# Expert weight sums formed once, ahead of time, and kept in DRAM, with deeper buffers for the expert weights

## The chip, the cores and the metric

The kernel runs on one core of a Trainium2 chip. The engines of the core are named as the profile names them: PE (TensorE; PEld is its weight load), DVE (VectorE), ACT (ScalarE), POOL (GpSimd) and SP (SyncE, which here only issues DMA transfers). The metric is the device time of one execution in microseconds (us), and less is better.

## The reference, cut to what matters

```python
attn = attention(q, k, v, mask from the nearest of 16 centroids)   # 2 x 8 heads, 768 tokens, head size 64
x = attn.transpose(0, 2, 1, 3).reshape(1536, 512)
x = softplus(x @ w_in) @ w_out                                     # w_in 512 x 2048
P = 8 rounds of Sinkhorn scaling of exp(x @ w_gate - max)          # 1536 x 8
for e in range(8):                                                 # the expert stage
    h = maximum(x @ w1[e], 0)                                      # w1[e] 512 x 1024
    out += P[:, e:e+1] * (h @ w2[e])                               # w2[e] 1024 x 512
```

## The kernel before

The program has three stages, one after the other. Attention comes first. It works through 8 pairs of heads in a list of events with hand-set step numbers (24 steps to a pair), and each pair is prepared ahead of its use: split into parts, compared with the centroids, and the cluster masks formed. The first feed-forward stage follows, in 16 units of 128 columns (`m1`, line 53). Then comes the expert stage, with 16 rounds k: 8 experts for each half of the tokens.

In the expert stage the tokens' matrix and each expert's weights are cut in 2 x 2 blocks and multiplied by the seven products of Strassen's method in Winograd's form. `PROD` (line 106) lists them: the token side is a block (A11...) or a sum of blocks (S1 to S4), the weight side a block (B11, B21, B22) or a sum (T1 to T4). Every operand is split into a high part that TensorE's fast 32-bit format holds exactly (`h`, a cast on ACT) and the rest (`l`, a subtraction), and each product takes three matmuls in place of one.

- First matrix (`x @ w1`): a round has four units u, each with 128 of the 512 half columns. `w1_load` (line 751) brings the four blocks of a unit to `wf`, one buffer of seven slots; `w1_sum` (761 to 763) forms T1 to T4 in it on POOL; `w1_split` (765) casts on ACT (`whA`, `whB`, `whC`, line 770) and subtracts on DVE (`wlA`, `wlB`, `wlC`, line 771), in three pieces: A holds B11 and B21, B holds T1 and T2, C holds the rest. `l1_group` (827) does the matmuls of one product (line 843, tiles `l0m`, `l1m`, `l3m`), copies partial sums out of PSUM on ACT (`c00m`, `c22m`, `c03m`, line 852) and adds on DVE (`XA`, line 862).
- Second matrix (`h @ w2`): `w2_load`, `w2_sum` (POOL, line 795), `w2_split` (ACT line 800, POOL line 801, tiles `vh` and `vl`), `g_split` for the token side (`gh`, `gl`, lines 821 and 822), and `l2_piece` for the matmuls (line 878, tiles `Y`).

The order is set by a list of events: `do(t, fn)` gives each step a time in units of one product of the first matrix (28 to a round), and the steps are written out sorted by it. The recording layer then moves instructions on each engine, by priorities and its own estimate of what is ready. At run time each engine works through its own row strictly in order, SP with its DMA issues too; a semaphore holds an instruction until its operands are there and its target is free. The loads of a unit stand 7.5 and 6.4 units ahead of its first product.

In attention `pair_argmax` (line 365) forms the cluster masks of a pair: DVE, then POOL (`A`, line 379), DVE, POOL (`OH`, line 387), and `pair_ohT` (390) transposes them on PE (`po`, line 394).

## Time and profile before

| | |
|---|---|
| median of 3 runs | 1773.78 us (1773.32 to 1778.39) |
| the profiled execution's own time | 1769.33 us |
| its span, first to last instruction | 1767.5 us |
| busy share of PE, DVE, ACT, POOL | 89%, 74%, 56%, 55% |
| mean granted TensorE clock | 0.958 of full speed |
| read from and written to HBM | 93.44 MB and 3.15 MB |

Time outside the span is 1.8 us. The busy shares are means over three stages with different limits, so the rows further down are taken by stage.

### The profile page before, as it was taken

How to read it: one execution, taken by the hardware profiler on the slowest of the kernel's cores; microseconds unless marked ns; L12 is line 12 of the kernel's file. 1: busy time of each engine (PE TensorE's matmuls, PEld its weight loads, DVE VectorE, ACT ScalarE, POOL GpSimd, SP SyncE). 2: the span in 40 equal slices, each digit the busy share in tenths (PEclk: the TensorE clock that was granted, in tenths of full speed). 3: DMA queues.
4: the chain of work that ended last, by engine and by line, in shares of the span. 5: the costliest groups of instructions: out<-in, count | busy, mean ns of one | idle time of the engine just before them, and what ended most of it. 6: DMA issues, size and time to landing. Idle time of an engine off the chain costs nothing.

```text
span 1767.5 us, 26385 instructions
## 1 busy us (share of the span) xinstructions
PE 1565.5 (89%) x9873; PEld 1488.7 (84%) x9873; DVE 1305.2 (74%) x1899; ACT 997.4 (56%) x1822; POOL 976.3 (55%) x760
## 2 busy tenths in 40 slices
PE   5899998999999988888988889878888988888798
PEld 4788887999997788888988888777888988888798
DVE  5899988876636788776766767877676777667678
ACT  4788887665654545455544545544555454554454
POOL 3323243211223357767667766775767677677676
PEclk8999999999999999999998999899999999999999
DMA  7564410311200111212111111112211112111110
GB/s 203 156 163 136 96 27 25 119 56 65 72 19 13 47 55 54 66 55 60 55 54 60 58 62 55 42 60 84 66 54 60 54 54 66 54 60 54 55 54 37
DMA packets 127985, 118.74 MB, mean 67 GB/s; under 512 B 6896, under 2 KB 115568, under 8 KB 127856
## 3 DMA queue, kind: packets, MB, share of 16 engines
q1 hardware_dynamic: 127712, 116.99, 22.3%
q8 instruction: 77, 1.26, 0.3%
q14 instruction: 52, 0.43, 0.1%
q10 hardware_dynamic: 144, 0.07, 0.0%
HBM read 93.44 MB, written 3.15 MB: 55 GB/s over the span
## 4 chain that ended last, share of the span: by engine, by line
PE 37%; POOL 23%; DVE 14%; DMA 10%; issue 9%; ACT 7%; SPq 0%; DVEq 0%; POOLq 0%; ACTq 0%
POOL wf L763 11%; DMA wf<-in_moe_w_dram 9%; PE y L639 7%; PE p L605 7%; POOL vl L801 5%; POOL w2t L795 4%; PE l0m L843 4%; PE av L507 3%; PE s L452 2%; PE t L492 2%; POOL w2r L795 2%; PE l3m L843 2%; PE Yb0m L878 2%; DVE gl L822 2%; PE Ya0m L878 2%
## 5 line engine op out<-in xcount | busy, mean ns | idle before, releaser
L763 POOL TENSOR_TENSOR wf<-wf 128x256 f32<-128x256 f32 x256 | 255.0, 1016 | 102.3 <-DMA wf<-in_moe_w_dram 50.4
L801 POOL TENSOR_TENSOR vl<-w2r,vh 128x512 fp32r<-128x512 f32 x128 | 205.5, 1607 | 171.4 <-ACT vh L800 171.4
L822 DVE TENSOR_TENSOR gl<-XA,gh 128x768 fp32r<-128x768 f32 x160 | 200.9, 1257 | 71.8 <-ACT gh L821 71.5
L801 POOL TENSOR_TENSOR vl<-w2t,vh 128x512 fp32r<-128x512 f32 x96 | 154.7, 1612 | 128.5 <-ACT vh L800 128.2
L770 ACT CAST whAm<-wf 128x512 fp32r<-128x512 f32 x64 | 39.6, 619 | 260.5 <-DMA wf<-in_moe_w_dram 258.1
L821 ACT CAST gh<-XA 128x768 fp32r<-128x768 f32 x160 | 133.6, 835 | 76.0 <-PE Yb1m L878 38.9
L771 DVE TENSOR_TENSOR wlAm<-wf,whAm 128x512 fp32r<-128x512 f32 x64 | 46.8, 732 | 152.4 <-ACT whAm L770 152.3
L878 PE MATMUL Ya0m<-vh,gl 128*128 128x256 f32 x512 | 146.1, 285 | 1.4 <-DVE gl L822 1.4
L878 PE MATMUL Ya0m<-vl,gh 128*128 128x256 f32 x512 | 145.7, 285 | 0.0
L878 PE MATMUL Ya0m<-vh,gh 128*128 128x256 f32 x512 | 145.6, 284 | 0.0
L843 PE MATMUL l3m<-chS,whCm 128*128 128x384 f32 x128 | 52.1, 407 | 83.1 <-ACT c03m L852 83.1
L864 ACT ACTIVATE XA<-XA 128x768 f32<-128x768 f32 x96 | 81.0, 845 | 63.8 <-DVE XA L862 63.8
L878 PE MATMUL Yb0m<-vh,gh 128*128 128x256 f32 x384 | 110.0, 287 | 2.3 <-DVE x L896 2.3
L878 PE MATMUL Yb0m<-vh,gl 128*128 128x256 f32 x384 | 110.2, 287 | 0.7 <-DVE gl L822 0.7
L878 PE MATMUL Yb0m<-vl,gh 128*128 128x256 f32 x384 | 110.1, 287 | 0.0
L499 DVE TENSOR_TENSOR el<-t,eh 128x384 fp32r<-128x384 f32 x192 | 102.4, 549 | 9.9 <-ACT eh L495 8.7
L771 DVE TENSOR_TENSOR wlCm<-wf,whCm 128x768 fp32r<-128x768 f32 x64 | 78.9, 1233 | 40.5 <-ACT whCm L770 40.2
L460 DVE TENSOR_REDUCE sc<-s 128x1 f32<-128x768 f32 x96 | 91.1, 950 | 20.0 <-PE s L452 19.8
L495 ACT CAST eh<-t 128x384 fp32r<-128x384 f32 x192 | 91.2, 480 | 20.8 <-PE t L492 11.8
L843 PEld LDWEIGHTS l3m<-chS,whCm 128*128 128x128 f32 x128 | 27.4, 214 | 88.7 <-ACT c03m L852 88.5
L795 POOL TENSOR_TENSOR w2t<-w2r,w2t 128x512 f32<-128x512 f32 x64 | 99.1, 1549 | 5.4 <-DMA w2r<-in_moe_w_dram 1.7
L492 PE MATMUL t<-idf,E 128*128 128x128 f32 x576 | 97.6, 276 | 4.7 <-ACT OHT L400 2.8
(242 smaller groups left out, 5790.2 us busy)
## 6 DMA issues: line engine op xcount, KB each, us to landing
w2r<-in_moe_w_dram SPq DMA_DIRECT2D x64, 512.0 KB, 3.6
wf<-in_moe_w_dram SPq DMA_DIRECT2D x128, 256.0 KB, 2.7
AT<-HL SPq DMA_DIRECT2D x64, 192.0 KB, 3.9
r<-in_moe_w_in_dram SPq DMA_DIRECT2D x16, 512.0 KB, 4.4
r<-in_moe_w_out_dram SPq DMA_DIRECT2D x16, 512.0 KB, 4.3
Bt<-HL SPq DMA_DIRECT2D x32, 192.0 KB, 3.8
rT<-in_qt_dram SPq DMA_DIRECT2D x8, 384.0 KB, 3.2
rT<-in_kt_dram SPq DMA_DIRECT2D x8, 384.0 KB, 3.7
```

Source lines behind the costliest of these rows:

```text
L492: nc.tensor.transpose(pt[:, t * P : (t + 1) * P], Et[i, t][:, s * P : (s + 1) * P], idf)
L499: nc.vector.tensor_tensor(el, TT.pop((i, s)), EHL[i, s].bitcast(F32), ALU.subtract)
L605: nc.tensor.matmul(ps, wt[:, s_, ks], xx[:, k_, :], start=n == 0, stop=n == 6 * nk - 1)
L639: nc.tensor.matmul(o_, wt[:, q, ms], gt[:, cols], start=first and i == 0 and st, stop=last and i == 2, skip_group_check=True,)
L763: nc.gpsimd.tensor_tensor(wf[:, SLOT[name], :], wf[:, SLOT[a], :], wf[:, SLOT[b], :], ALU.subtract)
L771: nc.vector.tensor_tensor(l, src, h.bitcast(F32), ALU.subtract)
L795: nc.gpsimd.tensor_tensor(W2R[name][p], W2R[a][p], W2R[b][p], ALU.subtract)
L801: nc.gpsimd.tensor_tensor(l, src, h.bitcast(F32), ALU.subtract)
L821: nc.scalar.copy(h, src)
L822: nc.vector.tensor_tensor(l, src, h.bitcast(F32), ALU.subtract)
L843: nc.tensor.matmul(ps, wt[:, s_, ks], xx[:, k_, :], start=i in (0, 1, 3) and n == 0, stop=n == 3 * nk - 1, skip_group_check=True,)
L878: nc.tensor.matmul(ps, g[:, v, ts], w[:, v, :], start=i in (0, 1, 3) and p == 0 and v == 0 and n == 0 and t != 1, stop=p == 1 and v == 1 a ...
```

## The change

The sums T1 to T4 depend on the weights alone, and the kernel before forms them in every round. The new version forms them once. `t_load` brings the four blocks of one expert and unit to a tile `ts`, `t_sums` makes T1 to T4 in place with four subtractions on POOL, and `t_store` writes them to a DRAM tile (`TD[0]` for w1, `TD[1]` for w2). There are 32 such groups for w2, in attention (one every 4.9 steps from step 24 on), and 32 for w1, in the first feed-forward stage (one every 3.2 products).

In the expert stage `w1_load` and `w2_load` then read blocks from the inputs and sums from the DRAM tiles. The raw weights of the first matrix have two buffers (`WR[0]` in `wf`, `WR[1]` in new tiles `w1r`), loaded 12, 11 and 10 units ahead; those of the second have four half buffers in turn. The subtraction of piece C (`wlC`) goes from DVE to POOL. Nothing else in the expert stage's arithmetic changes.

```diff
@@ new, ahead of the first feed-forward stage's helpers
+    def t_load(pool, m, e, u):
+        t = TS[m, e, u] = slot_pool[pool].tile([P, 4, KC // 2 * P], F32, tag="ts", name=f"ts{m}_{e}_{u}", bufs=TSB[pool])
+        for fh in range(2):
+            o = fh * (FE // 2) + u * P
+            if m:
+                nc.sync.dma_start(t[:, 2 * fh : 2 * fh + 2, :].rearrange("p s d -> p (s d)"), w2[e, o : o + P, :])
+            else:
...
+    def t_sums(m, e, u):
+        t = TS[m, e, u]
+        b11, b12, b22, b21 = (t[:, n, :] for n in ((0, 1, 3, 2) if m else (0, 1, 2, 3)))
+        for o_, u_, v_ in ((b11, b12, b11), (b12, b22, b12), (b22, b22, b11), (b21, b21, b22)):
+            nc.gpsimd.tensor_tensor(o_, u_, v_, ALU.subtract)
+
+    def t_store(m, e, u):
+        nc.sync.dma_start(TD[m][e][u], TS.pop((m, e, u)))
+
+    TSB = {"ap": 3, "fp": 2}
@@ in attention's events
+    for n in range(E * NF2):
+        e, u = divmod(n, NF2)
+        t = 24 + 4.9 * n
+        at(t, lambda e=e, u=u: t_load("ap", 1, e, u), ("tl", 0))
+        at(t + 6, lambda e=e, u=u: t_sums(1, e, u), ("tq", 0))
+        at(t + 12, lambda e=e, u=u: t_store(1, e, u), ("tw", 0))
@@ the expert stage
-    def w1_sum(name):
-        a, b = BSUMS[name]
-        nc.gpsimd.tensor_tensor(wf[:, SLOT[name], :], wf[:, SLOT[a], :], wf[:, SLOT[b], :], ALU.subtract)
+        if ch == "A":
+            nc.sync.dma_start(
...
+        elif ch == "B":
+            nc.sync.dma_start(dst[0], TD[0][e][u][:, 0:4:2, :])
+        else:
...
+            nc.sync.dma_start(dst[0][:, 1:3, :] if len(dst) == 1 else dst[1], TD[0][e][u][:, 1:4:2, :])
...
-        nc.scalar.copy(h, src)
-        nc.vector.tensor_tensor(l, src, h.bitcast(F32), ALU.subtract)
+        n = 0
+        for src in WR[u % 2, ch]:
+            m = src.shape[1]
+            hs = h[:, n : n + m, :]
+            nc.scalar.copy(hs, src)
+            (nc.gpsimd if ch == "C" else nc.vector).tensor_tensor(l[:, n : n + m, :], src, hs.bitcast(F32), ALU.subtract)
+            n += m
...
-    def w2_sum(k, name, p):
-        a, b = BSUMS[name]
-        nc.gpsimd.tensor_tensor(W2R[name][p], W2R[a][p], W2R[b][p], ALU.subtract)
+        else:
+            n = TORD[1].index(name)
+            for u in range(NF2):
+                nc.sync.dma_start(dst[:, u, :], TD[1][e][u][:, n, :])
...
-                do(t0 - 7.5, w1_load, k, u, 0)
-                do(t0 - 6.4, w1_load, k, u, 1)
-                for n, name in enumerate(("T1", "T2", "T3", "T4")):
-                    do(t0 - 4.5 + 0.3 * n, w1_sum, name)
+                for ch, d in (("A", -12), ("B", -11), ("C", -10)):
+                    do(t0 + d, w1_load, k, u, ch)
...
+        for i in range(7):
+            b, i_ = divmod(7 * k + i - 4, 7)
+            do(split_at[b][2 * i_ + 1] + 0.15 if b >= 0 else -1, w2_load, k, i)
@@ in the first feed-forward stage
+    for m in range(E * NF2):
+        e, u = divmod(m, NF2)
+        for o, fn in ((0, lambda e=e, u=u: t_load("fp", 0, e, u)), (3, lambda e=e, u=u: t_sums(0, e, u)),
+                      (5, lambda e=e, u=u: t_store(0, e, u))):
+            tsum_at.setdefault(divmod(int(3.2 * m) + o, 7), []).append(fn)
```

Line numbers grow with the new functions: 770 becomes 814, 771 becomes 815, 852 becomes 896, 379 becomes 405, 387 becomes 413.

ACT's row in the expert stage before, from the first to the fourth product of a unit (`whAm_0` is piece A of the next round's unit 0, `whBm_3` piece B of unit 3, `c03m_2` the copy in unit 2):

```order
L852 COPY c00m_2_11013<-l0m_2_11006 128x384
L821 CAST gh_51_11079<-XA_1_10436 128x768
L800 CAST vh_51_11075<-w2r_6563 128x512
L852 COPY c22m_2_11064<-l0m_2_11006 128x384
L770 CAST whAm_0_11265<-wf 128x512
L770 CAST whBm_3_11139<-wf 128x512
L852 COPY c03m_2_11104<-l3m_2_11097 128x384
```

The same place in ACT's row of the new version:

```order
L896 COPY c00m_2_11671<-l0m_2_11664 128x384
L814 CAST whAm_0_11924<-wf 128x512
L865 CAST gh_51_11736<-XA_1_11091 128x768
L844 CAST vh_51_11732<-w2r_7202 128x512
L896 COPY c22m_2_11721<-l0m_2_11664 128x384
L814 CAST whBm_3_11797<-w1r_7205 128x512
L896 COPY c03m_2_11761<-l3m_2_11754 128x384
```

The two casts no longer stand side by side in front of `c03m`, `whA` stands three instructions earlier, and the two read from different buffers.

SP's row in the expert stage before, two units (`w2r` are the loads of the second matrix):

```order
L791 DMA w2r_6562<-in_moe_w_dram 128x4x256
L754 DMA wf<-in_moe_w_dram 128x4x128 x2
L791 DMA w2r_6563<-in_moe_w_dram 128x4x256
L754 DMA wf<-in_moe_w_dram 128x4x128 x2
L791 DMA w2r_6563<-in_moe_w_dram 128x4x256
```

The new version's row over most of a unit (`td` are the DRAM tiles with the sums):

```order
L801 DMA wf<-in_moe_w_dram 128x2x128
L805 DMA wf<-td_4_0_90 128x2x256
L839 DMA w2r_7203<-td_3_0_118 128x256
L839 DMA w2r_7203<-td_3_1_119 128x256
L839 DMA w2r_7203<-td_3_2_120 128x256
L839 DMA w2r_7203<-td_3_3_121 128x256
L792 DMA wf<-in_moe_w_dram 128x4x128
L797 DMA w1r_7205<-td_4_1_91 128x2x256
```

There are some three times as many issues, loads of the two matrices are interleaved, and `wf` and `w1r` take turns.

POOL's row in attention before, from the mask step `A` of one pair to what follows `OH`:

```order
L319 TENSOR_TENSOR HL_1810<-rT_1656,HL_1810 128x768
L379 TENSOR_TENSOR A_1575<-A_1575,wsel 128x384
L387 TENSOR_SCALAR OH_1808<-OH_1808 128x6x32
L49 TENSOR_SCALAR rw_1880<-sc_1542 128x384
L49 TENSOR_SCALAR rw_2132<-sc_1795 128x384
```

The same pair in the new version:

```order
L405 TENSOR_TENSOR A_1707<-A_1707,wsel 128x384
L200 TENSOR_TENSOR ts_2_1_1761<-ts_2_1_1761 128x256 x4
L344 TENSOR_SCALAR rT_1793<-rT_1793 128x768
L345 TENSOR_TENSOR HL_1902<-rT_1793,HL_1902 128x768
L345 TENSOR_TENSOR HL_1961<-rT_1795,HL_1961 128x768
L413 TENSOR_SCALAR OH_1956<-OH_1956 128x6x32
L49 TENSOR_SCALAR rw_2036<-sc_1673 128x384
```

Four sums, a scaling and both `HL` subtractions now stand between `A` and `OH`, where nothing stood before.

## Rows read from the trace of the kernel before

**Rows 1.** The page: span, and PE's busy time, share and instructions.

```profile
span 1767.5 us, 26385 instructions
PE 1565.5 (89%) x9873; PEld 1488.7 (84%) x9873; DVE 1305.2 (74%) x1899; ACT 997.4 (56%) x1822; POOL 976.3 (55%) x760
```

**Rows 2.** Busy time by stage; last columns: clock, DMA share, GB/s.

```profile
core 0: us, PE busy (x) PEld busy (x) DVE busy (x) ACT busy (x) POOL busy (x), PEclk, DMA share, GB/s
60.00:240.00 180.00, 166.56 (x1075) 149.66 (x1073) 167.21 (x307) 152.04 (x337) 54.97 (x61) 0.99 0.49 128
320.00:520.00 200.00, 200.00 (x1152) 188.09 (x1151) 128.07 (x217) 124.20 (x242) 44.24 (x34) 1.00 0.20 68
640.00:1720.00 1080.00, 937.81 (x6113) 918.62 (x6114) 784.29 (x991) 547.62 (x906) 758.84 (x553) 0.95 0.19 59
```

**Rows 3.** Matmuls of lines 843 and 878: duration ns, first and last start.

```profile
L843 PE MATMUL l0m<-chA,whAm x128: 333/338/689, 575.8 to 1716.4; 128*128 128x384 f32 x128
L878 PE MATMUL Ya0m<-vh,gh x512: 274/283/416, 600.5 to 1762.2; 128*128 128x256 f32 x171
```

**Rows 4.** Waits of PE, 640 to 1720 us: us in total, times, longest.

```profile
PE l3m L843 <- ACT c03m L852: 83.1, 27, 4.3
PE l0m L843 <- ACT XA L860: 28.9, 29, 2.7
PE l0m L843 <- DVE XA L862: 18.5, 17, 2.0
PE l3m L843 <- DVE XA L862: 8.9, 5, 3.1
```

**Rows 5.** The longest wait of ACT, 640 to 1768 us.

```profile
ACT whAm L770 <- DMA wf<-in_moe_w_dram: 256.6, 56, 7.9
```

**Rows 6.** Timeline of one such wait: start, duration, idle before in brackets.

```profile
991.85 5.65 POOL L763 TENSOR_TENSOR wf<-wf 128x256 f32<-128x256 f32 x4 [1.74 <-DVE gl L822]
1000.38 0.62 ACT L770 CAST whAm<-wf 128x512 fp32r<-128x512 f32 x1 [6.50 <-DMA wf<-in_moe_w_dram]
1001.42 0.47 ACT L852 COPY c03m<-l3m 128x384 f32<-128x384 f32 x1
1001.94 0.44 PE L843 MATMUL l3m<-chS,whCm 128*128 128x384 f32 x1 [2.95 <-ACT c03m L852]
```

**Rows 7.** Stretches in and behind another such wait; columns as in rows 2.

```profile
738.20:741.20 3.00, 0.36 (x4) 0.16 (x2) 1.01 (x2) 1.66 (x4) 0.00 (x0) 0.94 0.73 236
741.20:744.60 3.40, 3.40 (x13) 3.27 (x14) 2.44 (x4) 1.25 (x3) 2.95 (x2) 0.56 0.03 11
```

**Rows 8.** Timeline of PE at full clock: start and duration.

```profile
734.92 0.34 PE L843 MATMUL l3m<-chS,wlBm 128*128 128x384 f32 x1
735.10 0.28 PE L878 MATMUL Ya1m<-vh,gh 128*128 128x256 f32 x1
735.22 0.28 PE L878 MATMUL Ya1m<-vl,gh 128*128 128x256 f32 x1
```

**Rows 9.** The longest wait of SP's queue, 640 to 1720 us.

```profile
SPq L754 <- POOL wf L763: 438.4, 57, 10.3
```

**Rows 10.** Single operations: duration ns minimum/median/maximum, first and last start.

```profile
L763 POOL TENSOR_TENSOR wf<-wf x256: 720/745/1520, 491.5 to 1709.3; 128x256 f32<-128x256 f32 x128
L319 POOL TENSOR_TENSOR HL<-rT,HL x14: 1799/1832/2150, 22.1 to 201.8; 128x768 fp32r<-128x768 f32 x14
L499 DVE TENSOR_TENSOR el<-t,eh x192: 508/550/560, 34.8 to 284.7; 128x384 fp32r<-128x384 f32 x192
L822 DVE TENSOR_TENSOR gl<-XA,gh x160: 895/1133/2051, 595.4 to 1758.1; 128x768 fp32r<-128x768 f32 x160
```

**Rows 11.** DMA issues: count, KB each, median us to landing.

```profile
w2r<-in_moe_w_dram SPq DMA_DIRECT2D x64, 512.0 KB, 3.6
```

**Rows 12.** Timeline of one pair's masks in attention.

```profile
141.57 1.00 POOL L379 TENSOR_TENSOR A<-A,wsel 128x384 f32<-128x384 f32 x1 [0.49 <-DVE sc L473]
144.43 0.35 POOL L387 TENSOR_SCALAR OH<-OH 128x192 fp32r<-128x192 f32 x1 [1.86 <-DVE OH L384]
144.84 0.37 PE L394 MATMUL po<-idr,OH 128*64 128x128 f32 x3 [0.36 <-POOL OH L387]
```

More of the change, by code (lines that the diff above doesn't have):

```diff
@@ L174, in fetch_unit @@
         )
+    TD = [
+        [[tc.dram_tile([P, 4, KC // 2 * P], F32, name=f"td{m}_{e}_{u}") for u in range(NF2)] for e in range(E)]
+        for m in range(2)
+    ]
+    TS = {}
+    TORD = (("T1", "T3", "T2", "T4"), ("T1", "T3", "T4", "T2"))
+    def t_load(pool, m, e, u):
[5 more added lines that the diff above has]
+            else:
+                for j in range(2):
+                    nc.sync.dma_start(
+                        t[:, (0, 3, 1, 2)[2 * fh + j], :].rearrange("p (k f) -> p k f", f=P),
+                        w1[e, j * DM // 2 : (j + 1) * DM // 2, o : o + P].rearrange("(k p) f -> p k f", p=P),
+                    )
+    def t_sums(m, e, u):
[6 more added lines that the diff above has]
+    TSB = {"ap": 3, "fp": 2}
     WT = {}
@@ L185, in w1_use @@
     def w1_use(T):
-        res = {}
-        for name, s_ in SLOT.items():
-            for ch, base in CHUNK.items():
-                n = 3 if ch == "C" else 2
-                if ch in T and base <= s_ < base + n:
-                    res[name] = T[ch] + [s_ - base]
-        return res
+        return {name: T[ch] + [n] for ch in T for n, name in enumerate(MEMBERS[ch])}
     def split_unit(u):
@@ L210, in w2_ @@
             nc.gpsimd.tensor_tensor(w2l[:, c], w2f[c], w2h[:, c].bitcast(F32), ALU.subtract)
-        return [lambda: w1_("A"), lambda: w1_("C")], [lambda c=c: w2_(c) for c in range(2)]
+        return [lambda: w1_("A"), lambda: w1_("D")], [lambda c=c: w2_(c) for c in range(2)]
     att = ExitStack()
@@ new lines, in w1_load @@
+    def w1_load(k, u, ch):
+        e = k % E
+        if ch == "A" and u % 2 == 0:
+            for c_, b_ in CHUNK.items():
+                WR[0, c_] = [wf[:, b_ : b_ + (3 if c_ == "C" else 2), :]]
+        dst = WR[u % 2, ch]
+        if ch == "A":
+            nc.sync.dma_start(
+                dst[0].rearrange("p s (k f) -> p (s k) f", f=P),
+                w1[e, :, u * P : (u + 1) * P].rearrange("(k p) f -> p k f", p=P),
+            )
+        elif ch == "B":
+            nc.sync.dma_start(dst[0], TD[0][e][u][:, 0:4:2, :])
+        else:
+            o = FE // 2 + u * P
+            b22 = dst[0][:, 0, :]
+            nc.sync.dma_start(
+                b22.rearrange("p (k f) -> p k f", f=P),
+                w1[e, DM // 2 : DM, o : o + P].rearrange("(k p) f -> p k f", p=P),
+            )
+            nc.sync.dma_start(dst[0][:, 1:3, :] if len(dst) == 1 else dst[1], TD[0][e][u][:, 1:4:2, :])
@@ L959, in attention_moe_moe2 @@
             do(S0 + 7 + 2 * p, g_sum, k, "S4", p)
-        prev, first = split_at.get(k - 1, [-99] * 14), split_at.setdefault(k, [])
+        first = split_at.setdefault(k, [])
         for j in range(14):
```

77 lines of the change are left out of this document (28 added, 49 removed).

## The prediction

> **What bounds the kernel now.** The page gives a span of 1767.5 us with PE busy for 89% of it [rows 1]. That share mixes three stages, so the table by stage comes next [rows 2]. In the first feed-forward stage PE is busy for all of the 200 us shown, at full clock: nothing can be gained there. In attention PE and DVE both stand at 93%, and POOL is busy for 55 of 180 us. In the expert stage PE is busy for 938 of 1080 us, and the mean granted clock falls to 0.95. This stage lasts from 575.8 us to about 1763 [rows 3], some 1187 us, two thirds of the span.
>
> Its floor can be counted. Matmuls of 384 columns start about 0.175 us apart at full clock, those of 256 about 0.12 [rows 8]. A round has 28 products of 6 of the first kind, and 14 pieces of 18 of the second. Sixteen rounds make 2688 x 0.175 + 4032 x 0.12 = 954 us. So 233 us of the stage are something else, and the waits of PE say what: 83.1 us at `l3m` for the copy `c03m` on ACT, 28.9 at `l0m` for the activation `XA` on ACT, and 27.4 for `XA` on DVE [rows 4].
>
> The copy takes 0.47 us, so the question is what ACT does ahead of it, and one such wait shows it [rows 6]. POOL forms the sums of a unit from 991.85 to 997.50 us. SP has the next load of `wf` waiting for them, because it overwrites a block that they read. The load lands, and only at 1000.38 can ACT cast `whA`, after 6.50 us idle. `whB` and then `c03m` stand behind it in ACT's row, and PE waits 2.95 us. ACT waits so 56 times, 256.6 us in all [rows 5], and SP waits 438.4 us for the sums [rows 9]. The single `wf` buffer closes the loop: sums, load, cast, copy, matmul.
>
> The waits cost a second time. In such a wait the granted clock is 0.94, and in the 3.4 us behind it the mean granted clock is 0.56, so mostly the lower of its two levels (1.2 GHz), while PE is busy throughout [rows 7]. Over the stage the clock's mean of 0.95 is worth 0.05 x 1080 = 54 us.
>
> **The change part by part.** *Two buffers and early loads.* The loads for unit u now overwrite what unit u - 2 read, and stand 12 to 10 products ahead in place of 7.5 and 6.4. A product's share of a round is 1187/16/28 = 2.65 us, so piece A has (12 - 4.6) x 2.65, about 20 us, from issue to cast. A load of twice the size lands in 3.6 us [rows 11]. Nothing on POOL stands between load and load any more. SP's row has three times the issues, and each load of the second matrix waits in it for a `vl` of POOL that is done about when the row comes there; the 20 us cover that. I take all of the 83.1 us, and of the other 56.3 us those that come from the same cast: two thirds of DVE's 27.4 (DVE too has its subtraction `wlA` behind that cast), and a fourth of the 28.9. That is 83 + 18 + 7 = 108 us. The bounds are 0 (the wait only moves) and 139 (all of rows 4).
>
> *The clock.* The waits that go are the long ones (up to 4.3 us). I take 50 of the 54 us; bounds 0 and 54.
>
> *POOL in the expert stage.* The 256 sums `wf` (0.745 us or more each [rows 10]) and the sums of the second matrix go; 64 subtractions `wlC` come, at 1.83 us as POOL's `HL` of the same width, 117 us, or 2.15 at most, 138 us. POOL gets lighter on balance. `wlC` is needed four products after its cast may start, over 8 us even at the floor's pace, against 2 for the work and about 2 for a `vl` in front: covered, cost 0. Without that cover PE would wait some 2 us in each of 64 units, 128 us; that bound is kept as a rival.
>
> *Sums in attention.* The 32 groups hold 128 subtractions of 256 columns, 0.745 us each as `wf`, 95 us (92 to 195 by that row's ends). Attention makes 192 steps from 34.8 to 284.7 us [rows 10], 1.30 us a step, so a group every 4.9 steps comes every 6.4 us and takes 3.0 of them. POOL's share goes from 31% to 78%. That work alone fits. But the row has changed where it is tightest: today `OH` ends at 144.78 and PE's `po` starts at 144.84 [rows 12], with no slack. In the new row four sums (3.0 us), a scaling (about 1) and two `HL` (3.7) stand between `A` and `OH`, 7.7 us where now 1.86 are idle. The recording layer has moved `A` two steps forward (2.6 us), which leaves about 3 us of lateness for a pair. Four pairs have such a row, one of them with four more sums: 4 x 3 + 3 = 15 us, and 5 for transfers that come later. I take 20. The lower bound is 0, since PE's row also has 12 score matmuls (2.1 us) more ahead of `po`; the upper is 7.7 us for each of 8 pairs, about 60.
>
> DVE's own operations there: `el` reads PSUM and SBUF and takes 508 to 560 ns, although POOL is busy for a third of the time; `gl`, with both operands in SBUF, spreads from 895 to 2051 [rows 10]. So I add nothing for `el`. The Trainium skill (SBUF — State Buffer, "Who interferes with whom") says that a DVE instruction with at most one SBUF input does not contend with GpSimd, and one with two does. By it the price here is 0, and the trace agrees. Were `el` stretched as `gl` is (1133/895) for the added 47% of POOL's time, 192 x 0.55 x 0.27 x 0.47 = 13 us would come on top.
>
> *Transfers of the sums.* 33.5 MB in 32 x 6.4 = 204 us is 164 GB/s on top of 128 at a share of 0.49 [rows 2]. At the feed-forward stage's 0.20 for 68 that is 0.48 more, 0.97 in all: near full, but each transfer has several steps of lead. Nothing added; a tenth of 204 us as bound.
>
> *Sums in the feed-forward stage.* POOL is busy for 44 of 200 us there and DVE for 128, PE's row does not change: 3 us, bounds 0 and 15.
>
> The sum against the profiled execution's own 1769.3 us: - 108 - 50 + 20 + 3 = -135, so 1634. The median of the runs lies 4.5 us above that execution, 1639 by it. I say 1637.
>
> **The rivals.** *Attention pays much more* (POOL late in every pair, DMA near full). For it: POOL at 78% with its row in order; against: 22% is left. With the upper bounds 60 + 20 in place of 20 the time is 1697.
>
> *Half of the wait comes back*, since SP's row still runs in order and whatever holds a load of the second matrix holds `whA`, or `wlC` comes late on POOL. For it: the interleaved rows and three times the issues; against: 20 us of lead. Half of 158 lost gives 1716.
>
> *Everything goes*: all of rows 4 and attention for nothing. -139 - 54 leaves about 1578.
>
> *Slower.* POOL becomes what bounds attention: per pair (24 steps, 31.2 us) it has 9.5 + 4.9 x 3.0 = 24 us of work. If its waits in row order came to another 27 us, a pair would take 51, 20 us more, and eight pairs would eat the whole 158. It decides from there; 25 us more per pair gives 1637 - 20 + 200 = 1817. The 22% left speak against it.
>
> *The change doesn't do what it says*: `whA` waits as before, because SP never gets ahead; with attention's price, 1797.
>
> **How the numbers follow.** The forecast (1605 to 1670) has 0.62, dear attention 0.17, half the wait 0.11, everything 0.05, slower by either way 0.04, near no change 0.01. About 0.3% (5 us) is what a measurement of this kernel can tell from no change. Faster gets 0.95, the same 0.01, slower 0.04. The range runs from 1595 to 1705: it takes in the forecast, most of dear attention, and the near side of the half case.
>
> **What would show it.** Right: ACT's wait for `whA` under 40 us, PE's for `c03m` under 15, the clock of the expert stage at 0.98 or more, the stage some 1030 us long, no wait of SP for sums there, attention's end some 20 us later with PE waiting for `OH` at `po`. Wrong: a new wait in front of line 843 (for `wlC`, or ACT's `whA` on a DMA), or attention's pairs going from 31 to 35 us and more.

## The result and the profile after

The changed kernel takes **1685.93 us** (median of 4 runs, 1683.84 to 1686.74) beside 1773.55 us for the kernel before on the same chip: a ratio of 0.950, 95% interval 0.948 to 0.952. The forecast was 1637 us, range 1595 to 1705. So the sign and the range held and the size did not: 88 us came off where 136 were forecast. The profiled execution took 1686.74 us, with a span of 1684.9 us.

The page of the kernel after, beside [rows 1]: span, then busy time, share of the span and instructions of each engine.

```profile
span 1684.9 us, 27842 instructions
PE 1556.9 (92%) x9873; PEld 1472.5 (87%) x9873; DVE 1266.4 (75%) x1835; ACT 1006.4 (60%) x1854; POOL 830.8 (49%) x728
```

PE makes the same 9873 matmuls and is busy for 9 us less. Where the 83 us of span come from is a matter of the stages. The first fence gives them for the kernel before, cut at the starts of the first `p` and of the first `l0m` [rows 3] (attention, first feed-forward stage, expert stage), the second for the kernel after, cut at the same places. Columns as in [rows 2].

```profile
0.00:285.70 285.70, 248.69 (x1554) 222.16 (x1554) 243.10 (x451) 222.46 (x490) 90.57 (x115) 0.96 0.46 121
286.90:575.80 288.90, 279.92 (x1559) 256.78 (x1560) 188.38 (x298) 171.13 (x334) 72.00 (x52) 0.98 0.17 56
575.80:1763.40 1187.60, 1036.90 (x6763) 1009.72 (x6761) 872.51 (x1148) 602.66 (x996) 813.73 (x593) 0.95 0.18 57
```

```profile
0.00:333.60 333.60, 274.20 (x1554) 237.19 (x1554) 253.34 (x451) 224.84 (x490) 183.79 (x243) 0.90 0.69 204
334.80:675.80 341.00, 294.52 (x1558) 267.54 (x1559) 207.51 (x297) 169.97 (x334) 166.42 (x167) 0.93 0.49 152
675.80:1680.70 1004.90, 988.08 (x6763) 967.71 (x6761) 804.29 (x1085) 610.41 (x1028) 480.63 (x318) 0.99 0.38 115
```

The length of a stage less the busy time of PE is its idle time. So each stage's difference splits in two: idle time, and the busy time of the same matmuls, which is longer where the granted clock (third column from the end) is lower.

| stage | before | after | difference | of it idle | of it busy | forecast |
|---|---|---|---|---|---|---|
| attention | 285.7 | 333.6 | +47.9 | +22.4 | +25.5 | +20 |
| first feed-forward | 288.9 | 341.0 | +52.1 | +37.5 | +14.6 | +3 |
| expert | 1187.6 | 1004.9 | -182.7 | -133.9 | -48.8 | -158 |

Together -82.7 us; the spans differ by 82.6.

**The expert stage.** The waits of PE there, beside [rows 4] (us in total, times, longest):

```profile
PE l3m L887 <- DVE XA L906: 8.3, 8, 1.7
PE Yb0m L922 <- POOL vl L845: 2.5, 1, 2.5
...
PE l0m L887 <- ACT XA L904: 0.3, 1, 0.3
```

The 83.1 us for `c03m` are gone, and the 28.9 for `XA` on ACT are 0.3. The wait of ACT for `whA` in the same stretch, where [rows 5] had 256.6 us for a DMA:

```profile
ACT whAm L814 <- PE l1m L887: 36.3, 30, 1.7
```

ACT now waits for PE to have read the old `whA`, not for a load: the bound has turned round. The longest waits of SP's queue, where [rows 9] had 438.4 us for the sums:

```profile
SPq L839 <- POOL vl L845: 243.4, 106, 7.7
SPq L801 <- POOL wlCm L815: 179.5, 49, 7.1
```

SP still waits long, now for POOL's other work, but PE is idle for only 16.8 us in the whole stage: the loads have the lead that the change gave them. Only the waits of PE (the first fence) count.

**Attention and the first feed-forward stage.** The waits of PE from 60 to 333 us and then from 335 to 675 us of the kernel after:

```profile
PE s L478 <- ACT E L491: 13.4, 19, 1.3
...
PE po L420 <- POOL OH L413: 2.4, 2, 2.1
```

```profile
PE p L637 <- DVE gf L651: 41.6, 16, 7.0
```

Two things were to be explained. In attention the wait that the prediction named, `po` for `OH`, is there with 2.4 us only, and the longest is one of PE's own scores `s` for `E` on ACT, in which no sum takes part. In the first feed-forward stage PE waits 41.6 us for `gf` on DVE, an operation that the change doesn't touch (before, the same wait was 7.2 us). The experiments are about these two.

### The profile page after: what moved, and what is told of

It reads as the page before. It is cut to its first block, busy times and chain, and to the rows that moved or that the text cites. A ratio compares the mean times of both kernels' runs of the same rounds, so it can differ in the third digit from the quotient of the medians.

```text
span 1684.9 us, 27842 instructions
## 1 busy us (share of the span) xinstructions
PE 1556.9 (92%) x9873; PEld 1472.5 (87%) x9873; DVE 1266.4 (75%) x1835; ACT 1006.4 (60%) x1854; POOL 830.8 (49%) x728
## 5 line engine op out<-in xcount | busy, mean ns | idle before, releaser
L845 POOL TENSOR_TENSOR vl<-w2r,vh 128x512 fp32r<-128x512 f32 x224 | 356.9, 1594 | 459.1 <-ACT vh L844 413.9
L200 POOL TENSOR_TENSOR ts<-ts 128x256 f32<-128x256 f32 x256 | 203.5, 798 | 113.9 <-DMA ts<-in_moe_w_dram 83.6
L866 DVE TENSOR_TENSOR gl<-XA,gh 128x768 fp32r<-128x768 f32 x160 | 168.1, 1051 | 86.3 <-ACT gh L865 86.3
L865 ACT CAST gh<-XA 128x768 fp32r<-128x768 f32 x160 | 133.9, 837 | 114.6 <-PE Ya1m L922 97.6
L844 ACT CAST vh<-w2r 128x512 fp32r<-128x512 f32 x224 | 137.6, 615 | 9.2 <-PE y L671 5.9
L491 ACT ACTIVATE E<-s,sc 128x768 f32<-128x768 f32 x96 | 86.9, 905 | 30.9 <-DVE sc L486 27.2
L922 PEld LDWEIGHTS Ya0m<-vh,gl 128*128 128x128 f32 x512 | 97.5, 190 | 0.0
L922 PEld LDWEIGHTS Ya0m<-vh,gh 128*128 128x128 f32 x512 | 97.4, 190 | 0.0
L922 PEld LDWEIGHTS Ya0m<-vl,gh 128*128 128x128 f32 x512 | 97.3, 190 | 0.0
L518 PEld LDWEIGHTS t<-idf,E 128*128 128x128 f32 x576 | 78.0, 151 | 19.1 <-DVE el L525 7.5
L860 DVE TENSOR_TENSOR XS<-XA,XA 128x768 f32<-128x768 f32 x32 | 64.6, 2020 | 33.6 <-ACT XA L904 33.6
```

Of the source, the lines that this page charges most:

```text
L200: nc.gpsimd.tensor_tensor(o_, u_, v_, ALU.subtract)
L491: nc.scalar.activation(e.rearrange("p (a c) -> p a c", a=2), Et[i, t][:, :, 0:CB], AF.Exp, bias=sc[:, 0, j, t : t + 1], scale=1.0, accum_o ...
L518: nc.tensor.transpose(pt[:, t * P : (t + 1) * P], Et[i, t][:, s * P : (s + 1) * P], idf)
L844: nc.scalar.copy(h, src)
L845: nc.gpsimd.tensor_tensor(l, src, h.bitcast(F32), ALU.subtract)
L865: nc.scalar.copy(h, src)
```

## The experiments

The theory to begin with: in attention the loads, sums and stores have moved the recording layer's order, scores now stand bunched in PE's row, and that order costs the time, not POOL; in the first feed-forward stage the sums hold POOL's row while they wait for their loads, and what stands behind them (`w2l`, `wlBD`) holds DVE. The rivals: POOL's row itself is late (the prediction's own mechanism), or the transfers are late (DMA share 0.69 where it was 0.46, or SP's row).

Every run was set beside the kernel before on the same chip, in four groups, whose times of before are 1760.72, 1758.93, 1762.26 and 1765.02 us, 9 to 15 us under the 1773.55 beside which the change has its 0.950. The change itself was not run again in these groups, but stages that an edit leaves alone were: the first feed-forward stage of `held` and `held_nosums` takes 340.5 and 341.4 us (341.0 in the change), and attention in `ffn_late`, `w2l_dve` and `wl_dve` 333.8 to 336.2 us (333.6). So stage lengths compare across groups to some 3 us, though each comes from one profiled execution; ratios compare within a group, and with the 0.950 only to the 0.8% by which the times of before differ. Stage lengths in us, cut as above:

| run (group) | median us | ratio [95%] | attention | first feed-forward | expert |
|---|---|---|---|---|---|
| held (1) | 1697.6 | 0.963 [0.961, 0.966] | 348.1 | 340.5 | 1003.7 |
| sums_out (1) | 1618.52 | 0.918 [0.915, 0.921] | 317.0 | 293.1 | 1002.9 |
| ffn_late (1) | 1670.59 | 0.948 [0.946, 0.950] | 335.4 | 325.8 | 1002.2 |
| w2l_dve (1) | 1676.01 | 0.950 [0.947, 0.953] | 333.8 | 330.7 | 1005.1 |
| held_nosums (2) | 1657.84 | 0.941 [0.939, 0.944] | 304.7 | 341.4 | 1002.9 |
| pinned (2) | 1645.4 | 0.935 [0.932, 0.939] | 310.4 | 321.5 | 1003.4 |
| wl_dve (2) | 1670.81 | 0.948 [0.946, 0.951] | 336.2 | 324.4 | 1003.5 |
| two_buf (2) | 1671.17 | 0.949 [0.945, 0.952] | 286.9 | 287.9 | 1087.9 |
| fin_q (3) | 1653.42 | 0.939 [0.936, 0.942] | 316.3 | 330.0 | 1003.1 |
| fin_raw (3) | 1641.51 | 0.932 [0.929, 0.934] | 315.7 | 318.5 | 1003.1 |
| two_buf2 (3) | 1668.45 | 0.947 [0.944, 0.950] | 288.7 | 287.1 | 1087.6 |
| rows_set (4) | 1662.63 | 0.942 [0.938, 0.946] | 321.0 | 334.0 | 1003.5 |

### The sums taken out

```diff
-        for o_, u_, v_ in ((b11, b12, b11), (b12, b22, b12), (b22, b22, b11), (b21, b21, b22)):
+        for o_, u_, v_ in ():
```

> The changed kernel without the 256 subtractions on POOL that form the sums (the loads and the stores stay, so what is stored is not the sums). In attention PE's row stays but for some 100 of 1555 rows. If the order is to blame there, attention still ends at 325 to 335 us; if the work on POOL is, at 286 to 296 us; if the transfers are, at 325 to 335 us. In the first feed-forward stage: if sums that wait for their loads ahead of the subtractions w2l are to blame, the stage takes 288 to 300 us in place of 341; if the transfers are, 335 to 341 us. Whole kernel: order and queue 1635 to 1645 us, POOL in both stages 1590 to 1600 us, transfers in both 1686 us.

All loads and stores of the sums stay. The first feed-forward stage falls to 293.1 us, 4 us above before, though its DMA share is 0.56, and PE's wait for `gf` falls to 9.7 us. So there nearly the whole price (48 of 52 us) hangs on the sums, and the transfers by themselves cost next to nothing. In attention only 17 of the 48 us go. One row shows the pace of a pair: `x<-tmp,rb` of DVE, two in each pair, 16 in all. The fourth to the twelfth of them are taken here and below, so from the first start to the last are four pairs. In the kernel after and in `sums_out` (duration in ns, first and last start):

```profile
L549 DVE TENSOR_TENSOR x<-tmp,rb x9: 544/546/555, 108.4 to 264.7; 128x384 f32<-128x384 f32 x9
```

```profile
L549 DVE TENSOR_TENSOR x<-tmp,rb x9: 544/545/555, 109.7 to 263.4; 128x384 f32<-128x384 f32 x9
```

Before, the row runs from 108.0 to 234.3 us, so a pair takes 126.3/4 = 31.6 us. It takes 39.1 after, and 38.4 with not one sum on POOL. In these four pairs POOL's work is not what costs. Of the 17 us, 15 are the two pairs behind the stretch of these rows (31.7 and 23.1 us in place of 36.0 and 34.0).

What does cost there is seen in PE's row of the kernel after (start, duration, idle before in brackets):

```profile
153.41 0.61 PE L478 MATMUL s<-AT,AT 128*128 128x384 f32 x2 [0.99 <-ACT E L491]
...
154.82 0.62 PE L478 MATMUL s<-AT,AT 128*128 128x384 f32 x2 [0.44 <-ACT E L491]
...
156.46 0.61 PE L478 MATMUL s<-AT,AT 128*128 128x384 f32 x2 [0.66 <-ACT E L491]
```

Score follows score, and each waits until ACT has emptied a buffer of scores by its `E`; so the stretch goes at the pace of DVE's `sc` and ACT's `E`, about 1.5 us a score, while PE has nothing else next in its row. In the order of before other matmuls stand between two scores.

These waits are the smaller part of the 7 us a pair. The four pairs before, and then in `sums_out` (columns as in [rows 2]):

```profile
108.00:234.30 126.30, 118.37 (x777) 107.57 (x777) 118.30 (x215) 107.80 (x240) 37.89 (x42) 1.00 0.47 123
```

```profile
109.70:263.40 153.70, 136.66 (x780) 116.88 (x779) 121.49 (x214) 110.41 (x243) 39.43 (x44) 0.89 0.75 225
```

PE's idle time grows by 9 us, and the busy time of its matmuls by 18, at a granted clock of 0.89 in place of 1.00. That the many short waits brought the clock down was not shown apart.

### The order of before, held

```diff
+    HELD = {"PE": [...], "DVE": [...], "Activation": [...]}   (the order that before has)
+        for x, y in zip(row, row[1:]):
+            tc.add_manual_dep(y, x.name, DependencyInfo(DependencyClass.NoSync, ...))
```

The attention instructions of PE, DVE and ACT are put into the order of the kernel before, by edges that only order the recording; loads, sums and stores stay where they were.

> The changed kernel, but in attention the instructions of PE, DVE and ACT are issued in the order that they have in the kernel before; the loads, sums and stores stay. If the longer attention (its end at 333.6 us in place of 285.7) comes from the changed order, it ends at 286 to 296 us with PE's clock at 0.97 or more, and the kernel takes 1640 to 1650 us. If it comes from the time that the sums take on POOL, or from their transfers, it ends at 325 to 335 us and the kernel takes about 1686 us. The first feed-forward stage (341 us) and the expert stage (1009 us) should stay as they are by either.

The theory that the order alone is to blame falls: attention does not shrink to before's length, it grows to 348.1 us, beyond both of the ranges that had been expected. The row of the `x` now runs from 111.6 to 282.0 us, 42.6 a pair. The longest wait of PE is the one that the prediction had named:

```profile
PE po L420 <- POOL OH L413: 20.2, 5, 6.6
```

And the timeline of POOL shows it at work in one pair, with the `po` that waits (the last line, from the timeline of PE):

```profile
242.17 1.83 POOL L345 TENSOR_TENSOR HL<-rT,HL 128x768 fp32r<-128x768 f32 x1
243.95 6.23 POOL L200 TENSOR_TENSOR ts<-ts 128x256 f32<-128x256 f32 x8
250.14 0.99 POOL L405 TENSOR_TENSOR A<-A,wsel 128x384 f32<-128x384 f32 x1
251.09 2.52 POOL L200 TENSOR_TENSOR ts<-ts 128x256 f32<-128x256 f32 x3
253.59 0.51 POOL L49 TENSOR_SCALAR rw<-sc 128x384 f32<-128x384 f32 x1
254.17 0.35 POOL L413 TENSOR_SCALAR OH<-OH 128x192 fp32r<-128x192 f32 x1
...
254.58 0.53 PE L420 MATMUL po<-idr,OH 128*64 128x128 f32 x3 [6.64 <-POOL OH L413]
```

Eight sums stand ahead of `A` and three between `A` and `OH`. POOL is never idle from 242.17 on, and the eleven sums take 8.75 us of that chain, more than the 6.64 us for which PE stands; DVE waits for `A` at `mx` (10.3 us in all). So both theories hold half: before's order wants `OH` early, and the sums make it late; the layer's new order gives `OH` time by putting scores ahead, and costs 7 us a pair of its own instead.

### Before's order, without attention's sums

```diff
-        at(t + 6, lambda e=e, u=u: t_sums(1, e, u), ("tq", 0))
```

> The rows of PE, DVE and ACT held in attention as before (as in the run where they were held and attention ended at 348.1 us), loads and stores as there, but without attention's 128 subtractions on POOL (what is stored there is not the sums). If the time of the sums in POOL's row made the 62 us by which attention was longer there, it ends at 286 to 292 us; if the transfers did, at 330 us or later; if each has a part, between. The first feed-forward stage stays at 341 us. By the first reading the kernel takes 1635 to 1645 us.

This is `held` without attention's sums; its loads and stores stay. Attention falls from 348.1 to 304.7 us, so in before's order the sums, placed as they were, cost 43 us. The remaining 19 above before are no matter of pace: each pair is within 0.5 us of the same pair before, except two of 46.6 and 42.6 us, which are 20.1 longer together. Waits of ACT in this run:

```profile
ACT HL L336 <- DMA rawv<-in_v_dram: 8.6, 1, 8.6
ACT HL L336 <- DMA rT<-in_qt_dram: 6.2, 1, 6.2
```

The loads of the attention inputs stand in SP's row behind loads of blocks (line 188), which wait 27.6 us, in 20 times, for stores `td` to have landed. That is the third rival, transfers, and here it is SP's order that makes them late; whether the DMA engines' load has a part is seen in the next run.

### The sums put into POOL's idle places

```diff
+    POOL_ROW = [(91,1), (0,1), ... (-1,12), (17,3), (-1,4), ...]   (-1: so many sums)
```

`pinned` is `held` with POOL's row written out: its own operations in before's order, 12 sums behind `OH` and `rw` of a pair, 4 ahead of the second `VV`, none between `A` and `OH`; loads and stores are timed to fit, and the subtractions `wl` and `w2l` are on DVE (below).

> All sums kept, but POOL's row in attention is laid out by hand: PE, DVE and ACT hold the rows of before, POOL too, and the sums stand where POOL was idle before (twelve behind OH and rw, four in front of VV), with none between A and OH. In the first feed-forward stage the subtractions wl and w2l go to DVE, so that no buffer wf or w2f waits for POOL. If the place of the sums in POOL's row is the cause of both losses, attention ends at 288 to 298 us, the first feed-forward stage takes 290 to 300 us, and the kernel takes 1585 to 1605 us. If the sums' share of POOL as such is, or the transfers, attention ends at 315 us or later and the kernel takes 1620 us or more.

With all sums back, four pairs take 129.8 us, 32.5 a pair, 0.9 above before:

```profile
L549 DVE TENSOR_TENSOR x<-tmp,rb x9: 543/544/555, 119.0 to 248.8; 128x384 f32<-128x384 f32 x9
```

POOL does the same work here as in `held`, at 42.6 us a pair. So what costs is the place of a sum in POOL's row. Nor is it the load of the DMA engines, whose share is 0.86 in these four pairs (0.47 before). Attention is still 24.7 us longer than before (between the two ranges that had been expected; the first feed-forward stage, at 321.5 us, misses its 290 to 300). PE's waits show two of the stalls that are left, at 282 and at 82 us:

```profile
PE rb L512 <- POOL rw L49: 7.8, 2, 7.4
PE av L533 <- ACT eh L521: 9.8, 1, 9.8
```

The first is a `rw` behind sums in the last pair. In the other ACT stands 10.2 us at `HL`, ahead of `eh` in its row, for an `rT` that is late in SP's row, as in the run before.

### The first feed-forward stage: sums later, or DVE off POOL's row

```diff
 ffn_late:
-    TSB = {"ap": 3, "fp": 2}
+    TSB = {"ap": 3, "fp": 3}
-        ... (3, lambda e=e, u=u: t_sums(0, e, u)), (5, lambda e=e, u=u: t_store(0, e, u))
+        ... (6, lambda e=e, u=u: t_sums(0, e, u)), (8, lambda e=e, u=u: t_store(0, e, u))
 w2l_dve:
-            nc.gpsimd.tensor_tensor(w2l[:, c], ...)
+            nc.vector.tensor_tensor(w2l[:, c], ...)
 wl_dve, as w2l_dve and:
-            (nc.vector if u == (1, 0, 0, 0) else nc.gpsimd).tensor_tensor(l, src, ...)
+            nc.vector.tensor_tensor(l, src, ...)
```

> The changed kernel, with the sums of the first feed-forward stage formed 6 places after their load (3 before), stored at 8 (5 before), and three buffers in place of two, so that a sum finds its load landed when POOL comes to it. If sums that wait for loads ahead of w2l are to blame for the stage's 341 us, it takes 290 to 310 us and PE's waits for gf fall from 41.6 us to under 15; the kernel takes 1640 to 1655 us. If the sums' own time on POOL or their transfers are to blame, the stage takes 330 to 345 us and the kernel 1675 to 1690 us. Attention stays at 333.6 us.

> The changed kernel, with the subtractions w2l of the first feed-forward stage on DVE in place of POOL, so that no buffer w2f waits for POOL. If the waiting w2l is the link by which the sums hold DVE and then PE, the stage's 341 us fall to 305 to 325 (the shorter waits of wf for wlBD on POOL stay), and the kernel takes 1650 to 1672 us. If contention for the memory or the transfers are to blame, the stage takes 341 us or some us more, since DVE has 16 more units of w2l to do, and the kernel 1685 to 1700 us.

> The changed kernel with all of wl and w2l of the first feed-forward stage on DVE, nothing else. Attention stays at 333.6 us. If the two waits of DVE's conversion for POOL (wf for wlBD, w2f for w2l) are what is left of the stage's loss, it takes 290 to 305 us in place of 341, and the kernel 1636 to 1652 us. If the sums slow DVE by contention, it stays at 320 us or more and the kernel at 1665 us or more.

In the kernel after, this is how a load that is late reaches PE (timeline, 484 to 497 us):

```profile
484.91 3.19 POOL L200 TENSOR_TENSOR ts<-ts 128x256 f32<-128x256 f32 x4 [5.16 <-DMA ts<-in_moe_w_dram]
488.79 1.52 POOL L200 TENSOR_TENSOR ts<-ts 128x256 f32<-128x256 f32 x2 [0.69 <-DMA ts<-in_moe_w_dram]
490.28 1.26 POOL L236 TENSOR_TENSOR w2l<-w2f,w2h 128x512 fp32r<-128x512 f32 x1
491.57 0.93 DVE L119 TENSOR_SCALAR w2f<-cm 128x512 int32<-128x512 int32 x1 [8.88 <-POOL w2l L236]
495.57 0.55 DVE L651 SCALAR_TENSOR_TENSOR gf<-p,u 128x384 f32<-128x384 f32 x1
496.17 0.69 PE L637 MATMUL p<-chA,whA 128*128 128x384 f32 x1 [7.04 <-DVE gf L651]
```

ACT has `w2h` ready at 482.62, but `w2l` stands in POOL's row behind six sums, two of which wait for loads (61.5 us of such waits in the stage). DVE may not overwrite `w2f` before, stands 8.88 us, and `gf` and PE stand behind it. All three edits cut at that chain, and by the stage's length all three help, by 15, 10 and 17 us (325.8, 330.7 and 324.4 in place of 341.0). The ratios of the whole kernel can't confirm it (0.948, 0.950 and 0.948 beside 0.950, to the 0.8% said above). None comes near 289: the first two fall between what was expected by either reading, and `wl_dve` into the range set for contention (320 us or more). In `wl_dve` no `wl` or `w2l` of this stage is left on POOL, and the wait has gone elsewhere. ACT and SP's queue there:

```profile
ACT cm L117 <- DMA r<-in_moe_w_in_dram: 37.2, 6, 13.7
```

```profile
SPq L203 <- POOL ts L200: 105.3, 32, 5.8
```

The stores of the sums (line 203) wait in SP's row for POOL, and the loads `r` of this stage's own weights stand behind them.

### SP's row freed

```diff
 fin_q (pinned's attention, tail ordered so that rw precedes sums):
-    at(14, lambda: fetch_first(0), ("fr", 0))
+    at(30, lambda: fetch_first(0), ("fr", 0))
-        nc.sync.dma_start(TD[m][e][u], TS.pop((m, e, u)))
+        (nc.sync if m else nc.gpsimd).dma_start(TD[m][e][u], TS.pop((m, e, u)))
 fin_raw, fin_q's attention, stores on SP two steps later, and:
-        r1, r2 = fetch_raw(u[3], nm)
+        with tc.high_priority(400):
+            r1, r2 = fetch_raw(u[3], nm)
 rows_set, fin_q with fetch_first back at 14, SP's row in attention by hand, a group of sums every 3.0 products in place of 3.2, and here:
-                    nc.sync.dma_start(       (the loads of the sums' blocks)
+                    nc.gpsimd.dma_start(
```

All three have three `ts` buffers, late sums, and `wl` and `w2l` on DVE.

> The kernel with POOL's row laid out by hand (attention's end 310.4 us, first feed-forward stage 321.5), with its remaining stalls taken on. In attention its two long stalls (9.8 us at 82 us, where the next pair's loads rT stand in SP's row behind transfers of the sums, and 7.4 us at 282 us, where rw stands on POOL behind eight sums) should go, since the raw loads of the first feed-forward stage are issued 16 steps later and the last sums stand behind rw: attention ends at 290 to 298 us if the sums cost nothing where they stand, at 305 or later if they load POOL or the memory as such. In the first feed-forward stage the stores of the sums are issued by POOL itself, behind the sums, so that SP's row has no wait for sums ahead of the loads r; loads come 6 places ahead with three buffers. If ACT's wait for r (35 us) was what had taken the place of POOL, the stage takes 290 to 303 us; if not, 315 or more. The kernel: 1588 to 1605 us, else 1620 us or more.

> The same attention, with the stores of the sums still in SP's row in the first feed-forward stage, loads 6 places ahead with three buffers, and the loads r recorded with a higher priority. By the queue theory the loads r still stand behind stores that wait for POOL, but less: the stage takes 303 to 318 us, between the 321.5 and what the stores on POOL's queue give, and the kernel 1600 to 1618 us. If the transfers as such are the cause, both come out alike.

> All sums kept. Attention: PE, DVE and ACT hold the rows of before, POOL's sums stand where it was idle, and now SP's row is set by hand too: its own transfers in the order of before (the next pair's loads rT ahead of AT and Bt), a load or store of the sums only where its buffer or its sums are done by then. First feed-forward stage: wl and w2l on DVE, and both loads and stores of the sums are issued by POOL, so that SP's row holds only the loads r there, as before. If the losses of both stages come from in-order rows (POOL's, then SP's) and not from the sums' work or transfers as such, attention ends at 288 to 296 us without a stall of PE over 3 us, the first feed-forward stage takes 290 to 305 us with ACT's wait for r under 10 us, and the kernel takes 1586 to 1610 us, faster than all others here. If the transfers or the work as such cost the stages, attention ends at 302 us or later, the stage takes 312 us or more, and the kernel 1620 to 1645 us as with the other two kernels of this kind.

`fin_raw`, whose new edit brings the loads `r` forward in SP's row, has the lowest ratio of all kernels that form the sums, 0.932, far below the change's 0.950; `pinned`, with 0.935, is not clear of it. Its stage is 318.5 us, just above the 303 to 318 that had been expected and only 3 us under the 321.5 of `pinned`, and ACT still waits 26.6 us for `r`. `fin_q` is a miss: with the stores gone to POOL's queue, SP's row waits 71.2 us for them at the loads (line 191) instead, and ACT still waits 29.3 us for `r`; 330.0 us. In attention both lost at the start what they won at the end: the loads `r` moved to step 30 come late for ACT's `cm`, which kept its place in the held row. ACT waits 23.7 us there in `fin_raw`, PE 23.0, and the 310 of `pinned` was not bettered. With `fetch_first` back at 14, `rows_set` loses that time elsewhere, since its SP row stands 90.0 us at line 188 for stores to land: one pair takes 54.5 us (36.9 before), in which POOL stands 15.77 us for a late load of the sums ahead of `A` and DVE 10.47 us for `A`, and four more take 33.8 to 36.8 us (321.0 in all).

`rows_set` frees SP's row of the sums, and ACT no longer waits for an `r`. The stage is 334.0 us all the same, where 290 to 305 had been expected if the rows alone were to blame. DVE makes as many operations in it as in `wl_dve`. The stage's busy times in `rows_set` (columns as in [rows 2]):

```profile
322.00:655.00 333.00, 290.38 (x1552) 263.40 (x1553) 253.44 (x327) 170.98 (x335) 218.82 (x292) 0.94 0.45 154
```

In `wl_dve` the same 327 operations of DVE take 213.76 us, 39.7 less, with POOL busy for 130.69 (in `rows_set` it issues the transfers as well). The timelines of POOL and DVE show how:

```profile
395.25 5.59 POOL L200 TENSOR_TENSOR ts<-ts 128x256 f32<-128x256 f32 x8
395.51 5.88 DVE L120 SCALAR_TENSOR_TENSOR w2f<-r,w2f 128x512 int32<-128x512 int32 x1
401.64 0.68 DVE L121 SCALAR_TENSOR_TENSOR w2f<-r,w2f 128x512 int32<-128x512 int32 x1
...
477.02 7.96 POOL L200 TENSOR_TENSOR ts<-ts 128x256 f32<-128x256 f32 x8
481.69 1.12 DVE L121 SCALAR_TENSOR_TENSOR w2f<-r,w2f 128x512 int32<-128x512 int32 x1
```

An operation that otherwise takes 0.69 us takes 5.88: it starts 0.26 us behind the start of the first of eight sums on POOL and ends 0.55 us behind the last. Eight operations of DVE in this stage took 2.7 to 6.3 us beside such runs, 41.1 us together, which is some 36 us more than their usual times and so most of the 39.7. PE feels it: its five longest idle stretches in the stage, 27 of its 43 us idle, end 0.5 to 3.1 us behind one of these eight each. It is not always so: in another run of eight sums, which itself took 7.96 us, DVE got six operations through at 0.96 to 1.23 us each (one is the last line). What decides between the two no run shows.

### The second buffer alone

```diff
+    def wfu(u):
+        return WFB[0] if u % 2 else wf
-                do(t0 - 7.5, w1_load, k, u, 0)
-                do(t0 - 6.4, w1_load, k, u, 1)
+                do(t0 - 12, w1_load, k, u, 0)
+                do(t0 - 11, w1_load, k, u, 1)
-                    do(t0 - 4.5 + 0.3 * n, w1_sum, name)
+                    do(t0 - 7.0 + 0.3 * n, w1_sum, u, name)
```

This is the kernel before with two `wf` and early loads; the sums stay on POOL in the expert stage. The room comes from `gh` and `gl`, three buffers in place of four, whose splits `two_buf2` puts 2.6 products later for the first three of a round. In both, one piece of the first round multiplies `S4` in place of `A12`; the instructions are the same.

> The kernel before with one part of the change alone: a second buffer wf of seven blocks for odd units, loads 12 and 11 products ahead and sums 7 ahead; the sums stay in the expert stage on POOL, nothing goes to DRAM (to make room the buffers gh and gl are three in place of four and their splits one piece later). If the expert stage's gain comes from the second buffer, it takes 1000 to 1030 us, attention and the first feed-forward stage stay at 285.7 and 289, and the kernel takes 1585 to 1620 us, less than the changed one. If it needs the sums out of POOL's row (POOL would be busy for some 80% of the shorter stage), waits for the sums stay: 1060 us or more, the kernel 1645 to 1760 us.

> The kernel before with a second buffer wf and early loads, sums on POOL in the expert stage, as in the run before of this kind, with the first three splits of a round 2.6 products later, so that the three buffers gh and gl are free when they are filled. The stage should take 1075 to 1095 us (1087.9 there), with PE waiting for XA on DVE and not for the copy on ACT, and the kernel 1655 to 1675 us. If the early refill of gh and gl made the waits there, the stage takes 1060 us or less.

The stage takes 1088 us in both, 100 less than before and 83 more than after, and attention and the first feed-forward stage stay within 3 us of before. As had been expected if the sums must leave POOL's row, it stays above 1060 us, though what PE waits for there is not the sums. By the ratios it is as good as the change (0.949 and 0.947 against 0.950), by the sum of the stages 17 us shorter: what the change gains over it in the expert stage, 83 us, it more than pays back in the other two, where it is 100 us longer. PE's waits in `two_buf`:

```profile
PE l0m L849 <- DVE XA L868: 36.4, 29, 2.3
PE l3m L849 <- DVE XA L868: 12.3, 14, 1.6
```

The wait for `c03m` is gone and 6.1 us for `XA` on ACT are left, so the buffer and the early loads, without the other parts of the change, open the loop of [rows 6]. What remains is mostly DVE. The group of `gl` in the expert stage, of `two_buf2` and then of the kernel after (busy us, mean ns | idle before):

```profile
L828 DVE TENSOR_TENSOR gl<-XA,gh 128x768 fp32r<-128x768 f32 x160 | 221.7, 1387 | 17.2 <-ACT gh L827 17.1
```

```profile
L866 DVE TENSOR_TENSOR gl<-XA,gh 128x768 fp32r<-128x768 f32 x160 | 168.1, 1051 | 86.3 <-ACT gh L865 86.3
```

The same 160 operations, both operands in SBUF, take 336 ns more each beside POOL's sums. `two_buf` has `wlC` on DVE too, and its `gh` and `gl` have three buffers where the change has four; how the 83 us split between these and the sums was not tried.

## Why the prediction was right and where it was wrong

**Two buffers and early loads, -108 us: right in mechanism, a little small.** Idle time fell by 133.9 us, inside the bounds of 0 and 139. The signs came: no wait of ACT for `whA` on a DMA in place of under 40 us, none for `c03m` in place of under 15, no wait of SP for sums. The two waits for `XA`, of which the sum took 25 of 56, went almost wholly (8.6 left). `two_buf` shows why: buffer and early loads remove most of the ACT part (6.1 us left), but the DVE part is 48.7 us there, more than before, and goes only with the rest of the change. The prediction charged what it took of DVE's part to the cast alone.

**The clock, -50 us: right.** Busy time of the same 6763 matmuls fell by 48.8 us, at 0.99 in place of 0.95. The stage is 1005 us long, 51 above the 954 of its floor.

**POOL in the expert stage, 0: right.** PE never waits for `wlC`. The waits of SP that the prediction covered with 20 us of lead, for `vl` and `wlC`, are there and harmless.

**`el`, 0: right.** From 60 to 240 us it takes 551 ns in the mean (548 before), with POOL busy for 107 of the 180 us.

**Sums in attention, +20 us: the mechanism half right, the size too small.** 47.9 us, inside its bounds of 0 and 60. The step named `po` waiting for `OH`, and that is what before's order pays (`held`, 20.2 us). But the 12 scores moved ahead of `po` were taken as relief only. They are what the kernel after pays with: 7 us a pair even without sums (`sums_out`), some 2 of them idle, as bunched scores go at the pace of DVE and ACT, and 5 in longer matmuls at the lower clock. The wrong sign that the prediction had set, pairs of 35 us and more, came: 39.1. The prices of the two orders do not add, they replace each other, and the rest (19 us in `held_nosums`) is SP's row, where the prediction had 5 us for late transfers. Half of the 47.9 us is busy time of PE at a granted clock of 0.90 in place of 0.96, which the step had not counted.

**Sums in the feed-forward stage, +3 us: this is the step that failed.** It measured 52.1, outside its bounds of 0 and 15, and is 49 of the 52 us between the sum and the result (the other errors, +28 in attention and -25 in the expert stage, nearly cancel). The step argued from shares: POOL busy for 44 of 200 us, DVE for 128. It did not ask what stands behind a sum in POOL's row. [rows 2] could not tell it; the order could. `sums_out` gives 293.1 us with every transfer in place, so the sums carry it, and the runs show three ways: POOL's row (a sum that waits for its load holds `w2l` and `wlBD`, and with them DVE and PE), SP's row (a store that waits for a sum holds the loads `r`), and operations of DVE, most of them with both operands in SBUF, which POOL's sums lengthen. Each edit that closes one meets the next: 324.4 with the first closed (321.5 in `pinned`, with the same stage), 318.5 with the second eased too, 334.0 with both closed and transfers issued by POOL. Only the price of the first way, 10 to 17 us, is clear from these lengths; the second is seen as waits, and its price is not shown. The third is seen at work in the 334.0, in 27 of PE's 43 us idle; what the transfers issued by POOL add there, and whether they are what makes the sums run eight in a row, was not tried apart. Whether the sums could be free in this stage is open: no run that forms them brought it under 318.5.

That the range held is in part luck. With the expert stage at its forecast and the other two stages as measured the sum is 1711 us, above the 1705 of the range; and the room in the range had been kept for attention, while the larger part of the excess is the feed-forward stage's.

The transfers, taken at nothing, were rightly taken so where only the load on the DMA engines is meant (the first feed-forward stage of `sums_out` at a share of 0.56, four pairs of `pinned` at 0.86; the prediction had 0.97 for attention, where it was 0.76 from 60 to 240 us), wrongly where SP's row is meant.

## What to carry to other kernels

Work that is moved to an engine with idle time is paid by what stands behind it in that engine's row, and by what stands behind its loads and stores in the queue that issues them. A share of busy time says only that the work fits; before costing it at nothing, look for the instruction next in the row, whom it releases, and whether a wait for a load can come ahead of it. Where a recording layer decides the order, an edit on one engine reorders the others as well: hold their rows, and only then read what the edit itself costs.

## What the runs showed of the hardware

A run of eight subtractions on POOL, 5.59 us without a gap, stretched a DVE operation with both operands in SBUF from 0.69 to 5.88 us (`rows_set`), where the prediction's dearest case had been a factor of 1133/895; another such run, of 7.96 us, let six operations through at 0.96 to 1.23 us each. In the same stage `gf`, which reads `p` in PSUM and one operand in SBUF, never took more than 559 ns in 64 times, and `gl`, with the same width and both operands in SBUF, took 559 in the median and 6276 at most. But `wf<-cm`, with one operand, in SBUF, took 431 and 6135:

```profile
L709 DVE SCALAR_TENSOR_TENSOR gf<-p,u x64: 539/554/559, 331.3 to 639.1; 128x384 f32<-128x384 f32 x64
L712 DVE TENSOR_TENSOR gl<-gf,gh x64: 539/559/6276, 334.7 to 640.2; 128x384 fp32r<-128x384 f32 x64
L119 DVE TENSOR_SCALAR wf<-cm x14: 411/431/6135, 325.0 to 542.5; 128x512 int32<-128x512 int32 x14
```

The Trainium skill (SBUF — State Buffer, "Who interferes with whom") says that a DVE instruction with two SBUF inputs contends with a GpSimd instruction that reads SBUF, that one with at most one such input doesn't, outside what it calls the 2-port perf modes (a condition that the prediction left out), and that the shared ports are held as "an exclusive lock". The trace agrees for `gl` and `gf`, with 6276 against 559 ns. The 6135 ns of `wf<-cm` fit that rule only if it ran in such a mode, which no run here shows. That the block can outlast one GpSimd instruction of 0.70 us and hold for eight in a row is shown by this trace alone.

A DMA issued from POOL's queue occupies POOL itself, here for 0.72 us for a load of the sums' blocks and 0.59 for a store (`rows_set`; busy us, mean ns | idle before):

```profile
L191 POOL DMA_DIRECT2D ts<-in_moe_w_dram x123 | 88.5, 721 | 11.0 <-DMA td<-ts 8.5 <-issue 2.4
```

With the 32 stores (18.8 us) the transfers moved out of SP's row cost POOL 107 us of its own, beside some 95 us for the 128 sums that it forms there (0.745 us each [rows 10]).
